# Early attention with a third score buffer, and the MLP's first norms and weights in space of their own

## The chip, the core and the metric

The kernel runs on one core of one Trainium2 chip. Five engines take their instructions in order, each from its own queue: PE (TensorE, matrix products and transposes), DVE (VectorE), ACT (ScalarE), POOL (GpSimd) and SP (SyncE, which issues nearly all DMAs). SBUF is the on-chip memory; PSUM, with eight banks, takes what PE produces. The metric is the device time of one execution in microseconds.

## The reference

Three layers follow each other, in float32, for 4 batches of 576 tokens:

```
scores = q k^T / 8                  # 4 batches x 8 heads, 576 x 576, head size 64
scores below (row maximum - tau) are masked; softmax; times v     -> x (4, 576, 512)
u  = x + real(fft over tokens and channels of x)
un = layer norm of u (no weights)
x  = u + relu(un @ w_ch1) @ w_ch2                                 # 512 -> 2048 -> 512
theta = x @ w_theta
u  = x + w_tok_r (x cos theta) + w_tok_i (x sin theta)            # mix over tokens
out = u + relu(u @ w_ch)
```

The MLP's and the last layer's weights come as float64.

## The kernel before

**Precision.** Most products use a float32 operand split in a high part (rounded to the matmul's format) and a low part (the rest), and add three products: high by high, high by low, low by high. So each operand costs an ACT copy (`hi`) and a DVE or POOL subtraction (`lo`).

**Attention.** The 32 heads are worked in 16 pairs. A pair's q and k are loaded (`raw`), split, and placed by 12 SBUF-to-SBUF DMAs in tiles L (q), H and X (high and low of k); each of `raw`, L, H, X has two buffers (`load_qk`, L293). A pair has 9 score tiles of 128 queries by 576 keys (`tile_ops`, L434). A tile goes: PE makes the scores in a PSUM buffer `ps` of two banks (L455, L456); DVE takes the negated maximum (L465); ACT the exponential (L470); DVE or POOL the bound, maximum less tau (L474, L476); DVE masks and sums (L481), after which `ps` is free; PE transposes the result (L488); ACT copies it from PSUM (L497). There are two `ps` buffers. All other PSUM results share four banks with the tag "O". When a pair's tiles are there, PE multiplies by v (L556) and DVE scales into `xT` (L561).

**Transform.** Each four pairs make one batch, whose two-dimensional transform (`fft`, L635) follows beside the next batch's pairs: POOL folds tokens and channels (L660 to L701; in the last batch the fold of the last pair may run on DVE), some extra rows go by DMA (L706), PE does two stages (L760 to L799), DVE joins them (L839, L843) and adds x (L817 to L821), and SP stores `u`. The last batch's transform has no later pairs beside it.

**MLP.** `channel_mlp` (L971) works 5 chunks of up to four 128-token tiles through 16 weight units. Chunk 0 is the tokens of batch 0, whose `u` is stored long before the pairs end. `norm` (L1068) loads a tile of `u`, DVE takes statistics (L1081, L1082), POOL the inverse root (L1086, L1087), DVE scales (L1091), PE transposes (L1096), ACT and DVE split (L1103, L1107). `widen` (L981) makes float32 of a unit of float64 weights by bit operations: ACT takes the magnitude of the high words (L999), DVE sets a floor (L1003), shifts and masks (L1007), sets the sign (L1011) and the low bits (L1015); ACT and POOL or DVE then split (L1034, L1037). A unit (`unit`, L1122) is 12 matmuls (L1134), relu and split (L1139, L1143) and a second product (L1154 to L1156) that adds into the two `ps` buffers.

**Space.** SBUF is handed over in three steps: when all pairs have their scores ("scores done"), the space of q and k becomes part "a" of the MLP's space; after the last pair ("attention done") part "b"; after the last transform ("fft done") part "c". The table `PART` (L1536) says which tile is in which part. The tiles of the norms (`un`, `bs`, `mv`), chunk 0's operands (`b16`, `b17`) and the buffers of the widening (`raw2`, `v0`, `v1`) are all in "a", so neither norms nor widening can begin before "scores done".

**Order.** The order on each engine is fixed when the program is built. `Plan` (L99) holds every operation with a cost, a priority and what it needs; `schedule` (L137) runs a model of the engines with these costs and picks, per engine, the lowest priority that can start. The engines then wait only on semaphores. `SHIFT` (L1552, L1671) is a long list of corrections that are added to priorities. Two operations that are listed in `PORT` for DVE and POOL are not put side by side.

Of the kernel before, what the change touches and what calls it, by code (L numbers as in the profile page):

```python
# [98 lines left out]
class Plan:  # L99
# [163 lines left out]

def attention_and_fft(pl, tc, ident, tb, pss, left, middle, right, qk, vv, cfk, cst, csr, u_d):
# [95 lines left out]
    def load_first():  # L360
# [7 lines left out]
        def dma(tag, h, o, n):  # L368
            def fn(e):
                for half, q in enumerate((e, nc.scalar)):  # L370
                    q.dma_start(loc[tag][64 * half:64 * half + 64, h * n:h * n + n], qk[0][64 * h:64 * h + 64, o:o + n])
            return fn
# [57 lines left out]
    def pair(p):  # L430
# [3 lines left out]
        def tile_ops(idx):  # L434
# [66 lines left out]
            ps, P, T = ("ps", k), ("P", (p, couple)), ("O", "T", k)  # L501
# [43 lines left out]
        def pv_ops(half, g):  # L545
# [3 lines left out]
            b, j = divmod(p, 4)  # L549
# [8 lines left out]
            def mul(e):  # L558
                if (j, half) == (0, 0):
# [9 lines left out]
            after = [("pv", k), ("Rc", p, half)] + ([("mu", p)] if half else []) + ([("mul", 4 * b)] if j else [])  # L569
            made = [xT] if (j, half) == (0, 0) else []  # L570
# [64 lines left out]
    def fft(b):  # L635
# [9 lines left out]
        def gtile(kind, j):  # L645
            return ("g1" if j else "g0", (b, kind, j))

        def mult(n, j):
            return (("POOL", pool(n)), ("DVE", dve(n))) if b == B - 1 and j == 3 else (("POOL", pool(n)),)

        def at(kind, j):
            return pr(9 * (4 * b + j) + FOLD_AT + "eo".index(kind), 10)
# [318 lines left out]
def channel_mlp(pl, tc, ident, tb, pss, P2, wf, u_d, x3_d, w3, w3_d):  # L971

    for t, n in dict(raw2=2, v0=1, v1=1, sh=1, un=2, hh=2, hl=2).items():
# [7 lines left out]
    def widen(key, src, n, prio):  # L981

        loc = {}
        vt = f"v{count[0] % 2}"
# [928 lines left out]
```

## Time and profile before

| what | us |
|---|---|
| median of 3 runs (lowest, highest) | 994.16 (993.51, 994.80) |
| the profiled execution, its own time | 994.31 |
| its span | 992.2 |
| PE busy | 957.0 (96%) |
| DVE busy | 643.3 (65%) |
| ACT busy | 445.4 (45%) |
| POOL busy | 219.2 (22%) |

The span runs from the first to the last instruction of the trace; busy time is the union of an engine's instructions, without its waits. The page cuts the span in 40 slices of 24.8 us; each digit is a busy share in tenths, 9 meaning 90% or more, and PEclk the granted TensorE clock in tenths of full speed. Score tiles run up to about slice 12, the end of the transforms and the start of the MLP lie in slices 13 and 14, the MLP reaches to about slice 31, and the last layer takes the rest.

### The profile page before, as it was taken

Reading aid. Unit: us, or ns where it says so; the run is one execution under the profiler, and the core shown is the slowest. Engines: PE = TensorE matmul, PEld = TensorE weight load, DVE = VectorE, ACT = ScalarE, POOL = GpSimd, SP = SyncE. Lnnn points to the kernel's source line nnn. Section 1 sums busy time; section 2 is a strip of 40 time slices with the busy share of each in tenths; the row PEclk is TensorE's granted clock in tenths of the full one; section 3 lists DMA queues with packets and bytes.
Section 4 is the critical chain, followed back from the end, with each engine's and each line's share of the span. In section 5 each row is a group of like instructions: output and inputs, shape, how many; then the busy total and the mean of one; then the engine's idle time right before and its main releaser. Section 6 shows DMA issues by size and latency. Waiting matters only on the chain.

```text
span 992.2 us, 16044 instructions
## 1 busy us (share of the span) xinstructions
PE 957.0 (96%) x5904; PEld 828.6 (84%) x5904; DVE 643.3 (65%) x1276; ACT 445.4 (45%) x845; POOL 219.2 (22%) x405
## 2 busy tenths in 40 slices
PE   6889999999999689999999999999999999999998
PEld 6667888887887578888888888898898999999998
DVE  6778888888888899985662442311255476776733
ACT  6678787787777344441331121111134333453410
POOL 3476565556454310021000000000000001100100
PEclk9999999999999899999999999999999999999999
DMA  7796656665652555555451461200316301111011
GB/s 191 199 229 163 184 147 167 181 161 147 151 134 83 168 178 172 180 188 183 172 191 38 156 209 54 75 1 1 127 55 245 106 23 52 40 35 57 23 37 48
DMA packets 49982, 122.86 MB, mean 124 GB/s; under 512 B 7089, under 2 KB 11761, under 8 KB 49521
## 3 DMA queue, kind: packets, MB, share of 16 engines
q1 hardware_dynamic: 48720, 117.84, 39.9%
q0 software_dynamic: 720, 2.76, 1.2%
q10 hardware_dynamic: 464, 1.25, 0.5%
q8 instruction: 47, 0.77, 0.3%
q14 instruction: 31, 0.25, 0.1%
HBM read 69.58 MB, written 23.66 MB: 94 GB/s over the span
## 4 chain that ended last, share of the span: by engine, by line
PE 86%; DVE 4%; DMA 4%; ACT 2%; issue 1%; SPq 1%; POOL 1%; DVEq 0%; POOLq 0%
PE h L1134 20%; PE y L1409 12%; PE acc L1155 7%; PE acc L1156 7%; PE acc L1154 7%; PE O L556 7%; PE f L1473 5%; PE th L1285 5%; PE T L488 4%; PE ps L455 4%; PE ps L456 3%; DMA raw<-in_qk 2%; ACT P L470 1%; DVE c L465 1%; DMA X<-raw 1%
## 5 line engine op out<-in xcount | busy, mean ns | idle before, releaser
L1134 PE MATMUL h<-uh,w 128*128 128x512 f32 (+1 forms) x640 | 198.5, 371 | 0.1
L1139 ACT ACTIVATE hh<-h 128x512 fp32r<-128x512 f32 (+1 forms) x80 | 44.4, 556 | 246.2 <-PE acc L1155 189.7
L1143 DVE SCALAR_TENSOR_TENSOR hl<-h,hh 128x512 fp32r<-128x512 f32 (+1 forms) x80 | 50.7, 636 | 146.0 <-ACT hh L1139 136.2
L1134 PEld LDWEIGHTS h<-uh,w 128*128 128x128 f32 x640 | 118.9, 188 | 17.4 <-issue 0.2
L470 ACT ACTIVATE P<-ps,c 128x576 f32<-128x576 f32 x144 | 106.6, 749 | 40.8 <-DVE c L465 37.9
L481 DVE SCALAR_TENSOR_TENSOR P<-ps,c,P 128x576 f32<-128x576 f32 x144 | 115.5, 814 | 13.4 <-ACT P L470 7.9
L465 DVE TENSOR_REDUCE c<-ps 128x1 f32<-128x576 f32 x144 | 106.8, 753 | 26.8 <-PE ps L456 25.0
L1134 PE MATMUL h<-ul,w 128*128 128x512 f32 (+1 forms) x320 | 118.4, 370 | 0.0
L1154 PE MATMUL acc<-w,hh 128*128 128x512 f32 x288 | 114.3, 397 | 0.0
L1156 PE MATMUL acc<-w,hl 128*128 128x512 f32 x288 | 113.2, 393 | 0.0
L1155 PE MATMUL acc<-w,hh 128*128 128x512 f32 x288 | 113.2, 393 | 0.0
L455 PE MATMUL ps<-H,L 128*128 128x288 f32 x320 | 99.3, 328 | 12.0 <-DVE P L481 10.9
L1409 PE MATMUL y<-w,z 128*128 128x288 f32 x768 | 110.6, 296 | 0.1
L1409 PEld LDWEIGHTS y<-w,z 128*128 128x128 f32 x768 | 104.6, 188 | 1.1 <-issue 0.3
L456 PE MATMUL ps<-X,L 128*128 128x288 f32 x320 | 89.4, 297 | 0.5 <-DVE X L403 0.5
L488 PE MATMUL T<-ident,P 128*128 128x128 f32 x576 | 82.2, 274 | 4.4 <-DVE P L481 1.9
L497 ACT COPY pt<-T 128x512 f32<-128x512 f32 (+1 forms) x160 | 82.3, 554 | 6.3 <-PE T L488 5.2
L556 PE MATMUL O<-pt,vr 128*64 128x320 f32 (+1 forms) x640 | 84.7, 411 | 0.0
L455 PEld LDWEIGHTS ps<-H,L 128*128 128x128 f32 x320 | 61.2, 191 | 24.4 <-issue 12.8
L488 PEld LDWEIGHTS T<-ident,P 128*128 128x128 f32 x576 | 67.4, 141 | 6.8 <-issue 1.9
L556 PEld LDWEIGHTS O<-pt,vr 128*64 128x64 f32 x640 | 43.1, 136 | 30.6 <-issue 3.7
L1134 PEld LDWEIGHTS h<-ul,w 128*128 128x128 f32 x320 | 60.1, 188 | 9.3 <-DVE ul L1107 0.3
(381 smaller groups left out, 1623.0 us busy)
## 6 DMA issues: line engine op xcount, KB each, us to landing
H<-hs SPq DMA_DIRECT2D x60, 160.0 KB
X<-raw SPq DMA_DIRECT2D x60, 160.0 KB
raw<-in_qk SPq DMA_DIRECT2D x14, 608.0 KB
vr<-in_vv SPq DMA_DIRECT2D x16, 384.0 KB
w<-w_d SPq DMA_DIRECT2D x6, 992.0 KB
mu<-u_d SPq DMA_DIRECT2D x18, 256.0 KB
ru<-u_d SPq DMA_DIRECT2D x18, 256.0 KB
x_d<-ru SPq DMA_DIRECT2D x18, 256.0 KB
```

The lines of the kernel that those rows point to most:

```text
L455: e.matmul(ps[:, half, :HS], L[:, qo:qo + 128], H[:, ko:ko + HS], start=(j == 0), stop=False)
L456: e.matmul(ps[:, half, :HS], L[:, qo:qo + 128], X[:, ko:ko + HS], start=False, stop=(j == n - 1))
L465: e.tensor_reduce(loc["c4"][:, 0:1], loc["ps"][:, :, :HS], axis=AXES.XY, op=ALU.max, negate=True)
L470: e.activation(halves(), loc["ps"][:, :, :HS], AF.Exp, bias=loc["c4"][:, 0:1], scale=1.0)
L481: e.scalar_tensor_tensor(halves(), loc["ps"][:, :, :HS], loc["c4"][:, 1:2], halves(), op0=ALU.is_ge, op1=ALU.mult, accum_out=st["sums"][:, ...
L488: e.transpose(T[:, kt * 128:(kt + 1) * 128], P[:, kt * 128:(kt + 1) * 128], ident[:])
L556: e.matmul(O[64 * h:64 * h + 64, :n], w, x, start=(kt == 0), stop=(kt == 4))
L1134: e.matmul(loc["ps"][:, :n], a, x[:, c, :n], start=(k == 0), stop=(k == 11))
L1154: e.matmul(a, hh[:, q], wh, start=(f == 0), stop=False)
L1155: e.matmul(a, hh[:, q], wl, start=False, stop=False)
L1156: e.matmul(a, hl[:, q], wh, start=False, stop=(f == NF - 1))
L1409: e.matmul(loc["ps"][:, half, :HS], z[:, cs], w, start=(n == 0 and m == 0), stop=(n == 8 and m == 2))
```

## The change

- Score tiles 0 to 35 (four pairs) have a third score buffer, `p2`: every third tile uses it. It is made of two of the four "O" banks, which are held until the mask of tile 35 and then given back (`two_more`).
- The pairs of each batch come in the order 3, 2, 1, 0 (`heads`), and with them the operations of the fold; the extra rows are taken from the pairs that now come first.
- A part "e" of SBUF is opened at the start. It holds the norms' tiles, chunk 0's operands and buffers `rawe`, `ve` for the first weight unit. The norms' loads no longer wait for "scores done"; the first unit's load waits for the first score tile of pair 12 in place of it. The descriptor space for POOL's DMAs is set to 1024.
- The widening has four steps for five: ACT scales the high words by 2^-112, POOL or DVE reduces the high word to its sign, DVE joins it with the low bits, DVE shifts and joins.
- The norm's scale may run on ACT, for which POOL makes one more value.
- The second block of `SHIFT` is replaced, so the planned order changes everywhere.

```diff
-        return self.banks[tag].tile(shape, F32, tag=f"{tag}{i}", name=name)
+        return (self.more if tag == "O" and i < 2 else self.banks[tag]).tile(shape, F32, tag=f"{tag}{i}", name=name)
...
+def heads(p):
+    return p + 3 - 2 * (p % 4)
...
-            e.dma_start(loc["raw"][:], qk[p])
...
+            third = 9 * p + idx < THREE and (9 * p + idx) % 3 == 2
...
-                ps = pss.tile([128, 2, 512], F32, tag="ps", name=f"ps{p}_{idx}")
+                ps = (pl.third if third else pss).tile([128, 2, 512], F32, tag="p2" if third else "ps", name=f"ps{p}_{idx}")
...
-            ps, P, T = ("ps", k), ("P", (p, couple)), ("O", "T", k)
+            ps, P, T = ("p2" if third else "ps", k), ("P", (p, couple)), ("O", "T", k)
...
-            b, j = divmod(p, 4)
+            b, j = divmod(heads(p), 4)
...
-            return ("g1" if j else "g0", (b, kind, j))
+            return ("g1" if j < 3 else "g0", (b, kind, j))
...
-            return (("POOL", pool(n)), ("DVE", dve(n))) if b == B - 1 and j == 3 else (("POOL", pool(n)),)
+            return (("POOL", pool(n)), ("DVE", dve(n))) if b == B - 1 and j == 0 else (("POOL", pool(n)),)
...
-            return pr(9 * (4 * b + j) + FOLD_AT + "eo".index(kind), 10)
+            return pr(9 * heads(4 * b + j) + FOLD_AT + "eo".index(kind), 10)
...
-            p0 = at(kind, j) + 0.02
-            pl.op(("ge", k), "SP", 1080, p0, extra, [("f2", (b, kind, j)), ("ez", b)], (),
+            p0 = at(kind, a) + 0.02
+            pl.op(("ge", k), "SP", 1080, at(kind, j) + 0.02, extra, [("f2", (b, kind, j)), ("ez", b)], (),
                   [g2, ex], delay=2500)
-            pl.op(("g", k), mult(ng, j), 0, p0 + 0.01, both, [("f2", (b, kind, j)), ("f2", (b, kind, a))], (), [g, g2])
+            pl.op(("g", k), mult(ng, a), 0, p0 + 0.01, both, [("f2", (b, kind, j)), ("f2", (b, kind, a))], (), [g, g2])
...
-            p0 = at("o", 3) + 0.02
-            pl.op(("ez", b), "POOL", 80, at("e", 2), extra_zero, (), [ex])
+            p0 = at("o", 2) + 0.02
+            pl.op(("ez", b), "POOL", 80, at("e", 3), extra_zero, (), [ex])
...
+THREE = 36
...
+        rt, vt = ("raw2", f"v{count[0] % 2}") if count[0] else ("rawe", "ve")
...
-            loc["raw"] = new("raw2", [128, 1024, 2], f"raw{key}", I32)
+            loc["raw"] = new(rt, [128, 1024, 2], f"raw{key}", I32)
...
-        def magnitude(e):
+        def rescale(e):
             loc["v"] = new(vt, [128, 1024], f"v{key}", I32)[:, :n]
-            e.activation(f32(loc["v"]), f32(loc["hw"]), AF.Abs)
-
-        def floor(e):
+            e.activation(f32(loc["v"]), f32(loc["hw"]), AF.Copy, scale=2.0 ** -112)
+
+        def sign(e):
+            h = f32(loc["hw"])
+            if e is nc.vector:
+                e.tensor_scalar(h, h, 0.0, None, op0=ALU.mult)
+            else:
+                e.tensor_mul(h, h, tb[:, 6:7].to_broadcast([128, n]))
+
+        def low(e):
+            e.scalar_tensor_tensor(loc["lw"], loc["lw"], 29, loc["hw"], op0=ALU.logical_shift_right, op1=ALU.bitwise_or)
+
+        def join(e):
             v = loc["v"]
-            e.tensor_scalar(f32(v), f32(v), 2.0 ** -15, None, op0=ALU.max)
-
-        def mantissa(e):
-            v = loc["v"]
-            e.tensor_scalar(v, v, 3, 0x3FFFFFF8, op0=ALU.logical_shift_left, op1=ALU.bitwise_and)
-
-        def sign(e):
-            v = loc["v"]
-            e.scalar_tensor_tensor(v, loc["hw"], -0x40000000, v, op0=ALU.bitwise_and, op1=ALU.bitwise_or)
-
-        def low(e):
-            v = loc["v"]
-            e.scalar_tensor_tensor(v, loc["lw"], 29, v, op0=ALU.logical_shift_right, op1=ALU.bitwise_or)
-
-        raw, v = ("raw2", key), (vt, key)
-        pl.op(("ca", key), None, 0, prio[0], begin, ["scores done"], [raw])
+            e.scalar_tensor_tensor(v, v, 3, loc["lw"], op0=ALU.logical_shift_left, op1=ALU.bitwise_or)
+
+        raw, v = (rt, key), (vt, key)
+        pl.op(("ca", key), None, 0, prio[0], begin, ["scores done"] if rt == "raw2" else [("S", (12, 0))], [raw])
         for i in range(2):
             pl.op(("cl", key, i), "SP", n * 1.55, prio[0], load(i), [("ca", key)], (), [raw], delay=2500)
-        pl.op(("c0", key), "ACT", act(n, False) + 80, prio[1], magnitude, [("cl", key, i) for i in range(2)], [v], [raw])
-        pl.op(("c1", key), "DVE", dve(n / 2), prio[2], floor, [("c0", key)], (), [v])
-        pl.op(("c2", key), "DVE", dve(n / 2), prio[2], mantissa, [("c1", key)], (), [v])
-        pl.op(("c3", key), "DVE", dve(n), prio[2], sign, [("c2", key)], (), [raw, v])
-        pl.op(("c4", key), "DVE", dve(n), prio[2], low, [("c3", key)], (), [raw, v])
+        pl.op(("c0", key), "ACT", act(n, False) + 80, prio[1], rescale, [("cl", key, i) for i in range(2)], [v], [raw])
+        pl.op(("c1", key), (("POOL", pool(n)), ("DVE", dve(n))), 0, prio[1], sign, [("c0", key)], (), [raw])
+        pl.op(("c2", key), "DVE", dve(n), prio[2], low, [("c1", key)], (), [raw])
+        pl.op(("c4", key), "DVE", dve(n), prio[2], join, [("c2", key)], (), [raw, v])
         return loc, v
...
-        pl.op(("wh", f), "ACT", act(1024, False), p0 - 1.5, hi, [("c4", ("w", f))] + (["fft done" if f >= NFA else "attention done"] if f else []), [slot],
+        pl.op(("wh", f), "ACT", act(1024, False), p0 - 1.5, hi, [("c4", ("w", f))] + (["fft done" if f >= NFA else "attention done"] if f else ["scores done"]), [slot],
...
+            e.tensor_scalar(mv[:, 1:2], mv[:, 0:1], -1.0, mv[:, 3:4], op0=ALU.mult, op1=ALU.mult)
...
+            if e is nc.scalar:
+                e.activation(u[:], u[:], AF.Identity, scale=mv[:, 3:4], bias=mv[:, 1:2])
+                return
             e.tensor_scalar(u[:], u[:], mv[:, 0:1], mv[:, 3:4], op0=ALU.subtract, op1=ALU.mult)
...
-        pl.op(("nl", k), "SP", 800, p0, load, ["scores done"] + stored(t), [u], delay=2500)
+        pl.op(("nl", k), "SP", 800, p0, load, stored(t), [u], delay=2500)
         pl.op(("n0", k), "DVE", 830, p0 + 1, stats, [("nl", k)], (), [u])
-        pl.op(("n1", k), "POOL", 820, p0 + 1, root, [("n0", k)])
-        pl.op(("n2", k), "DVE", 460, p0 + 2, scale, [("n1", k)], (), [u])
+        pl.op(("n1", k), "POOL", 985, p0 + 1, root, [("n0", k)])
...
-PART = {t: "a" for t in ("raw2", "v0", "v1", "un", "b16", "b17", "b0", "bs", "mv")}
+PART = {t: "a" for t in ("raw2", "v0", "v1", "b0")}
+PART.update({t: "e" for t in ("un", "b16", "b17", "bs", "mv", "rawe", "ve")})
...
 SHIFT += (
-    (('Rc', 13, 0), -94.12), (('Rc', 7, 1), -347.32), (('Rc', 8, 0), -290.69), (('Rc', None, 0), -37.05),
...
+    (('Rc',), -35.28), (('Rc', 14, 1), -54.55), (('Rc', 3, 0), -50.41), (('Rc', 7, 1), -115.81),
...
+    (('n0',), -20.29), (('n0', 0, 0), -904.08), (('n0', None, 0), -11.28), (('n3', 0, 2), -26.61),
+    (('n3', 2, 2), -15.94), (('n4',), -8.83), (('n4', 0, 0), -871.81), (('n5', 0, 1), -917.67),
...
             pl.tag("ps", 2)
+            pl.tag("p2", 1)
             pl.tag("O", 4, banks)
+            pl.third = top.enter_context(tc.tile_pool(name="third", bufs=1, space=PSUM, reuse_waits="tile"))
+
+            def two_more(e):
+                top.close()
+                pl.more = top.enter_context(tc.tile_pool(name="more", bufs=1, space=PSUM, reuse_waits="tile"))
+
+            held = [("O", "held", i) for i in range(2)]
+            pl.op("third", None, 0, -100, lambda e: None, (), held)
+            pl.op("two more", None, 0, -99, two_more,
+                  ["third"] + [("mask", divmod(n, 9)) for n in range(THREE) if n % 3 == 2], (), held)
             left, middle, right, late = Pools(tc, "left"), Pools(tc, "left"), Pools(tc, "right"), Late(tc, pl)
+            late.open("e")
             attention_and_fft(pl, tc, ident, tb, pss, left, middle, right, qk, vv, cfk, cst, csr, u_d)
...
             scores = [o["name"] for o in pl.ops if any(t[0] in RIGHT_TAGS for t in o["use"])]
...
-    nc = bacc.Bacc("TRN2", target_bir_lowering=False, num_devices=1)
+    nc = bacc.Bacc("TRN2", target_bir_lowering=False, num_devices=1, dynamic_dma_scratch_size=1024)
```

## Rows read from the trace of the kernel before

**Rows 1.** Stretches: us; busy us of PE, PEld, DVE, ACT, POOL; clock; DMA; GB/s.
```profile
0.00:25.00 25.00, 16.69 (x97) 15.74 (x98) 16.16 (x38) 15.85 (x28) 9.92 (x19) 0.93 0.73 192
25.00:75.00 50.00, 41.81 (x314) 32.63 (x313) 38.83 (x90) 35.52 (x70) 28.22 (x51) 1.00 0.88 214
75.00:125.00 50.00, 47.89 (x371) 38.57 (x369) 43.21 (x98) 39.69 (x86) 28.69 (x55) 1.00 0.69 174
125.00:325.00 200.00, 197.76 (x1554) 163.37 (x1554) 169.76 (x398) 152.00 (x321) 106.39 (x232) 1.00 0.57 148
325.00:375.00 50.00, 39.36 (x227) 34.12 (x226) 48.70 (x94) 20.52 (x33) 12.98 (x12) 0.90 0.52 167
375.00:975.00 600.00, 599.90 (x3252) 530.82 (x3251) 321.86 (x545) 180.84 (x307) 32.99 (x39) 1.00 0.30 100
975.00:992.20 17.20, 13.59 (x103) 13.36 (x102) 4.83 (x18) 0.95 (x4) 0.00 (x0) 1.00 0.16 52
```
**Rows 2.** Waits of PE, 0 to 100 us: us in total, times, longest.
```profile
PE ps L455 <- DVE P L481: 9.9, 8, 2.8
```
**Rows 3.** Waits of SP's queue, 0 to 110 us: total, times, longest.
```profile
SPq L332 <- PE ps L456: 10.7, 5, 7.8
```
**Rows 4.** The chain of waits, 0 to 110 us: start, length, what.
```profile
47.79 7.78 DMA L<-raw
55.58 7.94 DMA X<-raw
```
**Rows 5.** One line's instructions (L455), 25 to 75 us: PE, PEld, clock, DMA, GB/s.
```profile
25.00:75.00 50.00, 16.18 (x54) 9.93 (x53) 1.00 0.88 214
```
**Rows 6.** Waits of PE, 318 to 360 us, the longest.
```profile
PE xt L810 <- DVE dm L843: 4.7, 1, 4.7
```
**Rows 7.** Groups of DVE, 318 to 358 us: xcount | busy us, mean ns | idle before.
```profile
L1091 DVE TENSOR_SCALAR mu<-mu,mv 128x512 f32<-128x512 f32 x4 | 4.2, 1052 | 0.2 <-DMA raw('w', 0)_4626<-in_wf 0.2
L1081 DVE BATCH_NORM_STATS2 bs<-mu 128x6 f32<-128x512 f32 x6 | 4.1, 684 | 0.0
L1107 DVE TENSOR_TENSOR ul<-uT,uh 128x512 fp32r<-128x512 f32 x4 | 2.6, 679 | 0.0
...
L1011 DVE SCALAR_TENSOR_TENSOR v('w', 0)_4796<-raw('w', 0)_4626,v('w', 0)_4796 128x1024 int32<-128x1024 int32 x1 | 1.2, 1215 | 0.0
...
L1015 DVE SCALAR_TENSOR_TENSOR v('w', 0)_4796<-raw('w', 0)_4626,v('w', 0)_4796 128x1024 int32<-128x1024 int32 x1 | 1.2, 1192 | 0.0
...
L1007 DVE TENSOR_SCALAR v('w', 0)_4796<-v('w', 0)_4796 128x1024 int32<-128x1024 int32 x1 | 0.7, 686 | 0.0
```
**Rows 8.** The chain of waits, the first MLP matmul.
```profile
354.83 0.47 PE h L1134
```
**Rows 9.** Stretches of 2 us in the middle; columns as in rows 1.
```profile
332.00:334.00 2.00, 2.00 (x11) 1.92 (x10) 2.00 (x2) 0.12 (x1) 1.43 (x1) 0.50 0.29 66
...
342.00:344.00 2.00, 0.62 (x3) 0.62 (x4) 1.90 (x6) 1.98 (x2) 0.80 (x2) 0.50 0.44 129
344.00:346.00 2.00, 2.00 (x11) 2.00 (x10) 1.77 (x4) 0.00 (x0) 0.00 (x0) 0.50 0.97 340
346.00:348.00 2.00, 1.93 (x10) 1.53 (x9) 1.32 (x3) 0.38 (x1) 0.00 (x0) 0.50 0.52 195
```
**Rows 10.** DMA issues by POOL: count, KB each, median us to landing.
```profile
cfs<-in_cfk POOLq DMA_DIRECT2D x2, 516.0 KB, 7.2
...
ctr<-in_csr POOLq DMA_DIRECT2D x1, 640.0 KB, 9.5
```
**Rows 11.** Timeline, 337 to 341 us: start, length, instruction.
```profile
337.02 1.22 DVE L1011 SCALAR_TENSOR_TENSOR v('w', 1)_4816<-raw('w', 1)_4627,v('w', 1)_4816 128x1024 int32<-128x1024 int32 x1
337.54 2.91 POOL L1037 TENSOR_TENSOR w<-v('w', 0)_4796,w 128x1024 fp32r<-128x1024 f32 x1 [0.63 <-ACT w L1034]
338.15 2.58 DVE L1091 TENSOR_SCALAR mu<-mu,mv 128x512 f32<-128x512 f32 x1
```
**Rows 12.** Waits of DVE, 200 to 325 us.
```profile
DVE u L817 <- DMA u_d<-u: 2.5, 2, 2.0
```

More of the change, by code (lines that the diff above doesn't have):

```diff
@@ L370, in fn @@
                 for half, q in enumerate((e, nc.scalar)):
[L371 removed]
+                    q.dma_start(loc[tag][64 * half:64 * half + 64, h * n:h * n + n], qk[heads(0)][64 * h:64 * h + 64, o:o + n])
             return fn
@@ L558, in mul @@
             def mul(e):
-                if (j, half) == (0, 0):
+                if p % 4 == 0 and not half:
                     xTs[b] = new("xT", [128, 4, S], f"xT{b}")
@@ L568, in pv_ops @@
                   [("vr", p), ("pt5", p, 0), ("pt5", p, 1), (f"p0{half}", p), (f"p1{half}", p)])
-            after = [("pv", k), ("Rc", p, half)] + ([("mu", p)] if half else []) + ([("mul", 4 * b)] if j else [])
-            made = [xT] if (j, half) == (0, 0) else []
+            after = [("pv", k), ("Rc", p, half)] + ([("mu", p)] if half else []) + ([("mul", 4 * b)] if p % 4 else [])
+            made = [xT] if p % 4 == 0 and not half else []
             pl.op(("mul" if half else "mu", p), "DVE", dve(n), pr(g + 1, 7.5), mul, after, made,
@@ L669, in again @@
                 t = G["t", kind, j]
-                g = G[kind, j] = new("g1" if j else "g0", [128, 290], f"g{kind}{b}_{j}")
+                g = G[kind, j] = new("g1" if j < 3 else "g0", [128, 290], f"g{kind}{b}_{j}")
                 if kind == "e":
@@ L971, in channel_mlp @@
 def channel_mlp(pl, tc, ident, tb, pss, P2, wf, u_d, x3_d, w3, w3_d):
-    for t, n in dict(raw2=2, v0=1, v1=1, sh=1, un=2, hh=2, hl=2).items():
+    nc = tc.nc
+    for t, n in dict(raw2=2, rawe=1, ve=1, v0=1, v1=1, sh=1, un=2, hh=2, hl=2).items():
         pl.tag(t, n)
@@ L1111, in norm @@
         cs = [(a, ("c", ci)), (b, ("c", ci))]
-        pl.op(("nl", k), "SP", 800, p0, load, ["scores done"] + stored(t), [u], delay=2500)
+        pl.op(("nl", k), "SP", 800, p0, load, stored(t), [u], delay=2500)
         pl.op(("n0", k), "DVE", 830, p0 + 1, stats, [("nl", k)], (), [u])
-        pl.op(("n1", k), "POOL", 820, p0 + 1, root, [("n0", k)])
-        pl.op(("n2", k), "DVE", 460, p0 + 2, scale, [("n1", k)], (), [u])
+        pl.op(("n1", k), "POOL", 985, p0 + 1, root, [("n0", k)])
+        pl.op(("n2", k), (("ACT", act(512, False)), ("DVE", 460)), 0, p0 + 2, scale, [("n1", k)], (), [u])
         pl.op(("n3", k), "PE", 428, p0 + 3, turn, [("n2", k)] + ([("first", (ci - 2, NF - 1))] if ci > 1 else []) +
@@ L1750 @@
-    (('turn', None, None, 1), -6.3), (('turn', None, 'r'), -1.34), (('uh',), 84.74), (('us',), -104.35),
-    (('us', 1), 67.22), (('wl', 0), 54.14), (('x3',), 13.27), (('x3', 6), 43.93), (('x3s', 17), -9.75),
-    (('z',), 27.65),
[14 rows of a table added]
+    (('bound', 15, 7), -65.59), (('bound', 2), 38.66), (('bound', 5, 3), -52.26), (('bound', 6), -14.44),
+    (('bound', 6, 7), -53.12), (('bound', None, 1), 34.41), (('bound', None, 3), 15.7), (('bound', None, 4), -89.68),
[3 rows of a table added]
+    (('evac', None, 1), 83.37), (('exp',), -42.45), (('exp', 0, 5), -2.05), (('exp', 0, 6), 165.12),
@@ new lines @@
+    (('exp', 0, 7), 0.56), (('exp', 1, 8), 146.16), (('exp', 12, 3), 75.58), (('exp', 15, 1), 82.64),
+    (('exp', 2, 6), 44.13), (('exp', 3, 3), 39.1), (('exp', 3, 5), 0.9), (('exp', None, 3), 43.29),
[10 rows of a table added]
+    (('first',), 3.69), (('first', 0, 10), -28.82), (('first', 2), -23.47), (('fl',), 48.42),
[11 rows of a table added]
+    (('mask', 13, 2), 890.74), (('mask', 9, 5), 29.16), (('mask', None, 3), -27.12), (('mask', None, 5), -39.66),
+    (('mask', None, 6), 16.99), (('mask', None, 8), -11.78), (('mix',), 10.46), (('mix', 0, 0, (0, 1), 0), -29.7),
@@ new lines @@
+    (('mix', None, 1, (0, 1), 0), -8.66), (('mix', None, None, (0, 1), 3), 50.43),
+    (('mix', None, None, None, 1), -17.31), (('mix', None, None, None, 6), -20.32), (('mul', 12), -37.16),
[5 rows of a table added]
+    (('second', 2, 9), 33.13), (('second', 4, 4), 20.1), (('table',), 28.65), (('tk',), 31.54), (('tl', 0), -1.51),
+    (('tt',), 14.86), (('tt', 3), -32.21), (('turn', 0, 0), -33.48), (('turn', 1), 40.49), (('turn', 10, 6), 76.2),
+    (('turn', 10, 'r', 1), 25.85), (('turn', 10, 'r', 2), -16.69), (('turn', 11, 1), -3.58), (('turn', 11, 7), 77.35),
@@ new lines @@
+    (('turn', 11, 'r', 0), 16.46), (('turn', 12), -1.66), (('turn', 12, 3), -11.83), (('turn', 12, 4), 12.06),
+    (('turn', 13, 3), 1.06), (('turn', 13, 4), 886.61), (('turn', 14, 1), -1.71), (('turn', 14, 3), 27.2),
+    (('turn', 14, 4), 24.84), (('turn', 14, 8), 59.49), (('turn', 15, 4), 31.82), (('turn', 15, 'r'), 4.5),
+    (('turn', 2, 1), -0.71), (('turn', 2, 4), 22.73), (('turn', 3, 1), -16.45), (('turn', 3, 2), -9.96),
+    (('turn', 3, 5), 3.37), (('turn', 3, 6), 12.46), (('turn', 3, 8), 18.97), (('turn', 3, 'r', 1), 16.73),
@@ new lines @@
+    (('turn', 4, 4), 21.15), (('turn', 5), -0.64), (('turn', 5, 4), 20.36), (('turn', 5, 7), -18.52),
+    (('turn', 6, 6), 25.17), (('turn', 7, 'r', 2), -26.24), (('turn', 8, 2), -6.02), (('turn', 8, 3), -0.96),
+    (('turn', 8, 4), 16.16), (('turn', 8, 5), 38.27), (('turn', 9, 7), -28.1), (('turn', None, 0), 7.2),
+    (('turn', None, 1), -4.93), (('turn', None, 2), 0.49), (('turn', None, 4), 2.54), (('turn', None, 6), -1.59),
+    (('turn', None, 7), -2.48), (('turn', None, None, 2), -1.46), (('turn', None, 'r', 0), 30.44), (('uh',), 73.54),
@@ L1791, in body @@
             scores = [o["name"] for o in pl.ops if any(t[0] in RIGHT_TAGS for t in o["use"])]
-            attention = [o["name"] for o in pl.ops if any(t[0] not in LEFT_TAGS and t[0] not in ("ps", "O")
+            attention = [o["name"] for o in pl.ops if any(t[0] not in LEFT_TAGS and t[0] not in ("ps", "p2", "O")
                                                           for t in o["use"]) or o["name"][0] in ("guard", "inv", "Rt", "bound")]
```

44 lines of the change are left out of this document (13 added, 31 removed), and 92 rows, old and new, of the table SHIFT.

## The prediction

> **What bounds the kernel now.** I read the page, then its busy time in stretches, then the waits of PE, the chain of waits and the timeline of the two places where PE is not full. The stretches [rows 1] show a kernel that is bound by PE nearly everywhere: from 375 to 975 us PE is busy 599.90 of 600, from 125 to 325 it is busy 197.76 of 200. Nothing the change does in those stretches can gain much there; it can only lose. PE is idle for 8.31 us in the first 25, 8.19 from 25 to 75, 2.11 from 75 to 125, 2.24 from 125 to 325, 10.64 from 325 to 375, and 3.61 in the tail. That is 35.2 us in all and the whole prize, with what the clock takes beside it.
>
> At the start PE waits for a score buffer. In the first 100 us it stands 9.9 us, in eight waits, at the first score matmul of a tile until the mask of an earlier tile (DVE, L481) gives its PSUM buffer back [rows 2]. Two buffers serve a chain score, maximum, exponential, mask, and PE runs dry behind them. But the loads are near too: SP stood 10.7 us before the placing of a pair until the scores of an earlier pair let go of its tile L [rows 3], and the chain of waits holds 7.78 us for L and 7.94 us for X back to back [rows 4]. So one pair's placing takes at least 15.7 us (47.79 to 63.52), while in 25 to 75 PE did 54 of these matmuls, 20 a pair, so a pair took 18.5 us [rows 5].
>
> In the middle, 325 to 375, the last pairs are over, the last batch's transform is a chain across PE, ACT and DVE, and the MLP can't start. PE's longest wait is 4.7 us for a transform step on DVE (L843) [rows 6]. DVE is busy 48.70 of these 50 us [rows 1]: it also does chunk 0's layer norms and the widening of the first weight unit, which had to wait for the space of the scores [rows 7]. The first MLP matmul starts at 354.83 [rows 8]. Having run thin, PE was also slowed: the granted clock is 0.50 (1.2 of 2.4 GHz) in 332 to 334 and in 342 to 348 [rows 9].
>
> **The change part by part.** The sum is made against the profiled execution: 994.3 us, a span of 992.2 and 2.1 around it. The median of the runs shown, 994.16, lies 0.15 below, so both give the same forecast.
>
> (a) Third score buffer in the first 36 tiles, with two fewer banks for everything else. It can remove at most the 9.9 us of [rows 2]. It can't bring the next pair sooner than its placing: 18.5 less 15.7 is 2.8 us a pair, over the 2.5 to 3 pairs of that stretch 7 to 8 us. What is late next is that placing, and it itself starts when an earlier pair ends, so part comes back. Against it stand the two remaining banks: a transpose must wait until the copy before last has left, and a value product holds its bank until its multiply. No row shows two banks at work. I bound the part by 9.9 gained and, by the same eight waits moving from score buffers to these banks in all four pairs, 8 lost. I take a gain of 5, half of the waits, nearest to [rows 2].
>
> (b) Layer norms of chunk 0 and weight unit 0 leave the middle. The groups of DVE price them [rows 7]: statistics 0.68 each, so with the scale (4.2 for four) and the low part (2.6 for four) about 4 x 0.68 + 4.2 + 2.6 = 9.5, and the unit's four steps 0.7 + 0.7 + 1.2 + 1.2 = 3.8 (L1003 is as long as the L1007 shown). Some of the statistics were already done before 325, so about 11 us of DVE leave a stretch in which DVE is full. The last batch's steps then run when their inputs are there, and PE has unit 0 (twelve matmuls and a second half with as many columns) as filler in the gaps that remain. What can come back is the idle 10.64 and the clock: PE's busy time at 0.50 in [rows 9] is 2.00, 0.62, 2.00 and 1.93, half of which is 3.3. Together 13.9. The transform's chain itself stays and unit 1 still waits for the scores to end before it loads, so I leave 3.5 of it: a gain of 10.4. Bounds: 0, if these operations run no earlier, and 13.9.
>
> (c) The same work now lies in 125 to 325. There DVE has 200 - 169.76 = 30 us free and ACT 48 [rows 1], so 11 us fit by their sum, and the four groups of transposes only change place on a PE that is full in either. But each operation put ahead of a maximum or mask can hold PE for its own length, and PE has only 2.24 us of idle to swallow that. Between 0 and 11, I take 2, nearest to the large slack.
>
> (d) Widening in four steps instead of five. DVE loses two steps of 0.7 and keeps two of 1.2; the new sign step runs on POOL or, at about 1.2, on DVE. From 375 on PE is full, so there it is worth nothing; in 325 to 375 it is inside (b).
>
> (e) Pairs in the order 3, 2, 1, 0 of each batch. The extra rows of the transform are ready before the last pair. PE's longest wait in the middle is on DVE [rows 6], not on those rows, so 0; its most would be that 4.7, which (b) holds already. The smaller descriptor space: each table load takes 7.2 to 9.5 us from POOL's issue to landing [rows 10]. If POOL issues on as before it costs 0, which I take; if POOL were held until each landing, five loads hold it 4 x 7.2 + 9.5 = 38 us, 22 of them in POOL's idle time of 25 to 75 [rows 1], 16 beyond.
>
> Sum: 994.3 - 5 - 10.4 + 2 = 980.9, forecast 981.
>
> **A rule against it.** While POOL made the low part of unit 0 (2.91 us from 337.54, begun during a DVE step with two SBUF inputs), the DVE scale that began at 338.15 lasted 2.58 us, where the other three average (4.2 - 2.58) / 3 = 0.54 [rows 7, 11]. A POOL pass over 1024 columns thus can hold DVE for over 2 us. The Trainium skill, "SBUF — State Buffer", section "Who interferes with whom", says that a VectorE operation with two SBUF inputs and a GpSimd operation that reads SBUF exclude each other, whichever began second waiting; by that the sign step on POOL blocks the two remaining DVE steps, which both have two such inputs. The trace agrees for the scale; no row shows such a two-input step begun during a POOL read.
>
> **The rivals.**
> - POOL holds DVE in the middle. Of the units widened in 325 to 375 about five have a sign step on POOL, over 1024 columns as the 2.91 us row; if DVE waits for most of each, 11 us of DVE return, as much as (b) takes out, and of (b) about a third is left, the filler of unit 0: 994.3 - 5 + 2 - 3.4 = 988. For it: [rows 11]. Against it: what waits most in the hole reads PSUM.
> - The start gives nothing or a little less, because two banks or the placing take over: 986, up to 994 at the bound of (a). For it: [rows 3 to 5].
> - All comes back: 994.3 - 9.9 - 13.9 = 970.5. For it: the slack in [rows 1]; against it, the chain of the last batch.
> - Slower: the static order is held by loads that land late. In 125 to 325 DVE reads the four norm tiles and ACT two halves of weight unit 0 straight from new loads, and behind each in the queue stand the maxima, exponentials and masks on which PE waits. DVE already stood 2.5 us there, in two waits, for a store [rows 12]. A transfer among the pair loads took 7.78 or 7.94 us [rows 4]; a load that lands 3.5 us after its reader's turn costs that much of PE, and six cost 21: 994.3 - 15.4 + 21 = 1000. It decides from 15.4 / 6 = 2.6 us a load on.
> - Slower by (e): POOL held by the table loads, 981 + 16 = 997. No row shows the smaller space at work.
>
> **How the numbers follow.** Forecast 0.56; POOL holds DVE 0.14; nothing at the start 0.10; all 0.06; late loads 0.10; table loads 0.04. The predicted time is 981. The range 969 to 994 takes in the forecast's own terms, the first two rivals and part of the third, and leaves the slower cases out. A run can tell 0.2%, 2 us, from no change. Faster: the first four without the end of the second, 0.82; same 0.04; slower 0.14.
>
> **What would show it.** (a): the waits of score matmuls on masks in 0 to 100 at about half or less, PE idle in 0 to 125 near 13.5 instead of 18.6. (b): the first MLP matmul well before 340, PE busy in the 50 us after the last pair near 46, no granted clock of 0.50 there. (c): PE idle between 125 and the last pair under 5. (d): DVE steps of the widening no longer than 1.3. Wrong would be: DVE waiting for loads amid the pairs, waits of transposes on copies in the first four pairs, or a hole that only moved.

## The result, and the profile after

The changed kernel takes 984.38 us (median of 4 runs, 983.68 to 985.88), the kernel before beside it 994.3. The ratio is 0.9905, with a 95% interval of 0.9892 to 0.9917. The profiled execution took 984.21 us with a span of 982.1, 10.1 less than before. A second profile of the same kernel, in another comparison, has a span of 982.6 and a ratio of 0.9904 [0.9880, 0.9927].

The same stretches as in [rows 1], of the changed kernel (us; busy us of PE, PEld, DVE, ACT, POOL; granted clock; DMA; GB/s):
```profile
0.00:25.00 25.00, 17.08 (x95) 15.62 (x95) 16.62 (x39) 16.00 (x28) 9.17 (x20) 0.93 0.74 200
25.00:75.00 50.00, 46.06 (x341) 35.72 (x341) 41.84 (x101) 39.11 (x78) 28.49 (x48) 1.00 0.90 214
75.00:125.00 50.00, 48.97 (x377) 38.61 (x379) 41.23 (x95) 40.31 (x87) 34.70 (x62) 1.00 0.74 188
125.00:325.00 200.00, 193.61 (x1514) 161.41 (x1512) 174.23 (x413) 152.81 (x318) 114.41 (x236) 1.00 0.57 150
325.00:375.00 50.00, 48.10 (x281) 39.41 (x278) 42.59 (x66) 21.20 (x33) 16.36 (x13) 1.00 0.54 179
375.00:975.00 600.00, 599.33 (x3280) 531.15 (x3279) 298.73 (x510) 182.72 (x315) 58.73 (x59) 1.00 0.29 97
975.00:982.10 7.10, 3.50 (x27) 3.27 (x25) 1.57 (x6) 0.00 (x0) 0.00 (x0) 1.00 0.26 83
```
PE's idle time is each stretch less PE's busy time. Against [rows 1] it went from 18.61 to 12.89 us in the first 125, from 2.24 up to 6.39 in 125 to 325, from 10.64 to 1.90 in 325 to 375, and from 0.10 to 0.67 in 375 to 975. Together that is 9.75 less; PE's busy time is 0.35 less. These make the 10.1. The clock of 0.50 in the middle [rows 9] is gone (325 to 375 has 1.00).

The waits of PE in the first 100 us (total, times, longest) answer [rows 2]:
```profile
PE ps L460 <- DVE P L486: 4.6, 4, 3.5
PE T L493 <- ACT pt L502: 2.3, 6, 0.6
...
PE ps L460 <- DVE c L479: 1.2, 1, 1.2
PE R L601 <- ACT pt L502: 1.2, 2, 1.0
PE T L531 <- ACT pt L502: 0.9, 1, 0.9
```
The wait for a score buffer fell from 9.9 to 4.6 us, or to 5.8 with the 1.2 that the view puts down to the bound (L479), at the same matmul. In its place stand waits of a transpose for a bank that ACT has yet to copy out: 2.3, 1.2 and 0.9, where the kernel before had 0.8 and 0.7 of that kind in the same stretch. I put them down to the two banks that were given away; t27 below, which takes these back after three pairs, has no such wait in 62.5 to 125, where the changed kernel has 1.2. SP's wait to place a pair until the scores let go of L [rows 3] is now short:
```profile
SPq L336 <- PE ps L461: 3.3, 2, 2.9
```
The first MLP matmul, in the timeline (start, length), against 354.83 in [rows 8]:
```profile
329.98 0.48 PE L1142 MATMUL h<-uh,w 128*128 128x512 f32 x1
```

### The profile page after: what moved, and what is told of

It is laid out like the page before. It is cut to its first block, busy times and chain, and to the rows that moved or that the text cites. A ratio compares the mean times of both kernels' runs of the same rounds, so it can differ in the third digit from the quotient of the medians.

```text
span 982.1 us, 15994 instructions
## 1 busy us (share of the span) xinstructions
PE 956.6 (97%) x5904; PEld 825.2 (84%) x5904; DVE 616.8 (63%) x1226; ACT 452.1 (46%) x856; POOL 261.9 (27%) x436
## 4 chain that ended last, share of the span: by engine, by line
PE 83%; DVE 6%; ACT 5%; issue 2%; DMA 2%; POOL 1%; SPq 0%; DVEq 0%; ACTq 0%
PE h L1142 18%; PE y L1417 12%; PE O L561 7%; PE acc L1163 6%; PE acc L1162 6%; PE acc L1164 6%; PE f L1481 5%; PE th L1293 5%; PE T L493 4%; PE ps L460 4%; PE ps L461 3%; ACT P L475 2%; DVE c L470 2%; ACT pt L502 1%; DMA mu<-u_d 1%
## 5 line engine op out<-in xcount | busy, mean ns | idle before, releaser
L486 DVE SCALAR_TENSOR_TENSOR P<-ps,c,P 128x576 f32<-128x576 f32 x144 | 114.9, 813 | 10.7 <-ACT P L475 8.3
L1417 PE MATMUL y<-w,z 128*128 128x288 f32 x768 | 108.1, 295 | 0.0
L561 PE MATMUL O<-pt,vr 128*64 128x256 f32 (+1 forms) x640 | 84.7, 411 | 0.0
```

The costliest lines, as they stand in the source:

```text
L486: e.scalar_tensor_tensor(halves(), loc["ps"][:, :, :HS], loc["c4"][:, 1:2], halves(), op0=ALU.is_ge, op1=ALU.mult, accum_out=st["sums"][:, ...
L561: e.matmul(O[64 * h:64 * h + 64, :n], w, x, start=(kt == 0), stop=(kt == 4))
L1417: e.matmul(loc["ps"][:, half, :HS], z[:, cs], w, start=(n == 0 and m == 0), stop=(n == 8 and m == 2))
```

## The experiments

Each kernel starts from the changed one. "Planned anew" means that the program orders the operations afresh, with the corrections that were made for the changed kernel; "same order" keeps every engine's order.

**e2: the early start undone** (planned anew).
```diff
-load, stored(t), [u], delay=2500)
+load, ["scores done"] + stored(t), [u], delay=2500)
-["scores done"] if rt == "raw2" else [("S", (12, 0))]
+["scores done"]
```


> The loads of the norms and of weight unit 0 wait for the last score tile again, as in the kernel before; all else is the changed kernel, planned anew. If the early start is what filled the middle, PE's idle time in 325 to 375 goes from 1.90 back to 9 to 12 us, the first MLP matmul from 330 back to about 350, and the time to 992 to 996 (984.4 + 10, less the 2 to 4 that 125 to 325 gets back). If the hole closed for another reason (fewer widening steps, the order of the pairs), the first MLP matmul stays before 340 and the time within 2 us of 984. Either way 0 to 125 keeps its idle 12.9.

Measured: 999.93 us, ratio 1.0058 [1.0038, 1.0078], slower than the kernel before. The first MLP matmul starts at 364.96. The middle of e2, and the stretch before it:
```profile
325.00:375.00 50.00, 37.76 (x196) 31.80 (x193) 39.93 (x72) 22.50 (x34) 25.23 (x30) 0.80 0.50 169
125.00:325.00 200.00, 195.12 (x1522) 161.24 (x1519) 166.50 (x398) 147.09 (x310) 106.27 (x221) 1.00 0.54 142
```
The hole is back: 12.24 us idle for 1.90, and a granted clock of 0.80 on the mean. The clock costs nearly as much as the idle: PE's busy time over the whole run is 965.42 for 956.65, 8.8 more. So, under these corrections, the early start is a condition of the gain. My number was too small, since I had priced the idle and left out the time that PE then runs at the lower clock. Nor did 125 to 325 get back the 2 to 4 us that I had expected: it still idles 4.88 us, though the first of the moved statistics runs at 319.4.

**t9 and t27: the third buffer for one pair, and for three** (planned anew).
```diff
-THREE = 36
+THREE = 9        # t27: 27
```


> The third score buffer serves only the first 9 tiles (the first pair) instead of 36; planned anew. Theory: the buffer gains where pairs 1 and 2 run, so PE's idle time in 25 to 75 goes from 3.94 back to 7 to 9 and the time to 987 to 990. Rival: the gain of the start is made in the first pair, or by something else than the buffer (the order of pairs, later work pulled forward): idle in 25 to 75 stays under 5 and the time within 2 us of 984.4.

> The third score buffer serves the first 27 tiles (three pairs) in place of 36; planned anew. Theory: the buffer pays in the pairs in which it stands, so PE's idle in 25 to 62.5 is as in the changed kernel (2.8) and that of 62.5 to 100 grows from 2.1 by 2 to 4 (it was 4.2 in the kernel before); time 986 to 989. Rival: t9 lost its 13 us by a plan whose corrections fit another kernel; then the start here is either as in the changed kernel (0 to 125 idle near 12.9) or as poor as in t9 (27.0), whichever pairs have the buffer.

Measured: t9 999.45 us, ratio 1.0049 [1.0034, 1.0063]; t27 992.21, 0.9979 [0.9963, 0.9996]. Stretches of the kernel before, of the changed kernel, of t27 and of t9, in this order:
```profile
25.00:62.50 37.50, 32.17 (x242) 24.73 (x241) 29.20 (x69) 25.45 (x51) 19.61 (x34) 1.00 0.86 209
```
```profile
25.00:62.50 37.50, 34.66 (x252) 26.15 (x253) 29.95 (x72) 27.21 (x56) 19.57 (x33) 1.00 0.92 213
62.50:100.00 37.50, 35.37 (x268) 27.89 (x267) 32.99 (x80) 30.78 (x66) 25.46 (x45) 1.00 0.77 204
```
```profile
25.00:62.50 37.50, 35.23 (x256) 26.73 (x257) 30.05 (x71) 27.18 (x57) 19.88 (x35) 1.00 0.93 223
62.50:100.00 37.50, 32.12 (x240) 25.26 (x239) 27.74 (x68) 27.60 (x57) 23.43 (x46) 0.95 0.73 189
```
```profile
25.00:62.50 37.50, 29.57 (x219) 22.20 (x219) 27.68 (x65) 24.38 (x48) 13.63 (x19) 1.00 0.82 209
```
With the buffer in pairs one to three, t27 idles 2.27 us in 25 to 62.5, as the changed kernel does (2.84); t9, without it, idles 7.93. From 62.5 on, where t27 lacks it too, it idles 5.38 for 2.13. So the buffer pays in the pairs in which it stands. But its price can't be read off: t9 with two buffers is worse than the kernel before with two (5.33 in 25 to 62.5), so part of t9's loss, and I take it of t27's, is a plan whose corrections were made for three. That would explain why both expected times were too low; no run separates it.

**e5: every sign step on DVE** (same order).
```diff
-            if e is nc.vector:
-                e.tensor_scalar(h, h, 0.0, None, op0=ALU.mult)
-            else:
-                e.tensor_mul(h, h, tb[:, 6:7].to_broadcast([128, n]))
+            nc.vector.tensor_scalar(h, h, 0.0, None, op0=ALU.mult)
```


> Same order on every engine but for one thing: the sign step of all weight units is emitted on DVE, the ones that POOL had too. If POOL's sign step holds DVE's two widening steps, the shift-and-join steps of 2.83 and 2.10 us near 350 fall to about 1.2. Theory: those lie off PE's path in the middle and where PE is full, so the time stays within 1.5 us of 984.4. Rival (POOL holds DVE on PE's path): PE's idle 1.90 in 325 to 375 falls and the time drops by 2 us or more.

Measured: 982.63 us, 0.9878 [0.9861, 0.9895]; the profiled span is 982.1, that of the changed kernel. The timeline of the changed kernel at the sign step on POOL (L1013), then the same steps of e5:
```profile
347.13 3.00 POOL L1013 TENSOR_TENSOR raw('w', 4)_5006<-raw('w', 4)_5006,tb 128x1024 f32<-128x1024 f32 x1 [8.50 <-ACT v('w', 4)_5083 L1006]
347.15 1.20 DVE L1016 SCALAR_TENSOR_TENSOR raw('w', 3)_4910<-raw('w', 3)_4910 128x1024 int32<-128x1024 int32 x1
348.39 2.83 DVE L1020 SCALAR_TENSOR_TENSOR v('w', 3)_5050<-v('w', 3)_5050,raw('w', 3)_4910 128x1024 int32<-128x1024 int32 x1
```
```profile
350.34 0.68 DVE L1010 TENSOR_SCALAR raw('w', 4)_5006<-raw('w', 4)_5006 128x1024 f32<-128x1024 f32 x1
350.94 1.21 DVE L1017 SCALAR_TENSOR_TENSOR v('w', 3)_5050<-v('w', 3)_5050,raw('w', 3)_4910 128x1024 int32<-128x1024 int32 x1
```
DVE's join of unit 3 took 2.83 us beside POOL's step and takes 1.21 without it; POOL's own step took 3.00, where the shortest of this size took 1.92. The Trainium skill, "SBUF — State Buffer", section "Who interferes with whom", has the two exclude each other, and the trace agrees. Unit 4's join stayed at 2.10, beside POOL's low part of unit 3. PE doesn't feel it in the middle: its idle in 325 to 375 is 2.23, so the rival is out there. The time fell by 1.75 us, a little more than the 1.5 that my theory allowed; from 375 to 975 PE idles 0.09 for 0.67, and the profile, whose span is that of the changed kernel, explains no more. The intervals of the two ratios overlap, so that e5 is faster is not shown.

**e11 and e16: the old five steps, for all units, and for those after unit 7** (same order; the sign step's slot stays empty).
```diff
-e.scalar_tensor_tensor(loc["lw"], loc["lw"], 29, loc["hw"], op0=ALU.logical_shift_right, op1=ALU.bitwise_or)
+e.tensor_scalar(f32(v), f32(v), 2.0 ** -15, None, op0=ALU.max)
+e.tensor_scalar(v, v, 3, 0x3FFFFFF8, op0=ALU.logical_shift_left, op1=ALU.bitwise_and)
...
-e.scalar_tensor_tensor(v, v, 3, loc["lw"], op0=ALU.logical_shift_left, op1=ALU.bitwise_or)
+e.scalar_tensor_tensor(v, loc["hw"], -0x40000000, v, op0=ALU.bitwise_and, op1=ALU.bitwise_or)
+e.scalar_tensor_tensor(v, loc["lw"], 29, v, op0=ALU.logical_shift_right, op1=ALU.bitwise_or)
```


> Same order, but every weight unit is widened by the old steps: ACT takes the magnitude, POOL's or DVE's sign step is empty, and DVE does floor, mantissa (0.7 each), sign and low (1.2 each). Theory: four steps for five are worth nothing, since PE is full behind them: the time within 1 us of 984.4, PE's idle in 325 to 375 under 3 (1.90 with four). Rival: DVE is near its limit in the middle (42.6 of 50 us busy), and 0.7 to 1.4 us more for each of the seven units widened there brings back 3 us or more of idle and a time of 987 or more.

> Same order; units 0 to 7 of the weights are widened by the new four steps, all later units and the last layer's weights by the old five, with the sign step's slot empty. If the 10 us that e11 cost come from the middle, where DVE is full and the units 1 to 7 are made, this stays within 1.5 us of the changed kernel (0.990 of before). Rival: DVE supplies weights just in time up to 450 us, and the later units cost as well: 987 or more, with idle of PE between 385 and 450.

Measured: e11 994.25 us, 0.9992 [0.9976, 1.0007]; e16 984.66, 0.9902 [0.9879, 0.9925]. Stretches of e11:
```profile
325.00:375.00 50.00, 45.62 (x264) 37.24 (x264) 40.97 (x66) 19.59 (x31) 10.36 (x12) 0.97 0.47 157
375.00:385.00 10.00, 8.03 (x39) 6.78 (x40) 9.31 (x13) 4.13 (x5) 2.40 (x1) 1.00 0.46 155
342.00:344.00 2.00, 0.72 (x6) 0.39 (x4) 1.97 (x3) 0.13 (x1) 0.00 (x0) 1.00 0.37 131
344.00:346.00 2.00, 0.64 (x3) 0.64 (x4) 1.94 (x4) 0.91 (x1) 0.00 (x0) 0.73 0.58 117
346.00:348.00 2.00, 2.00 (x11) 2.00 (x11) 1.75 (x4) 0.95 (x1) 0.00 (x0) 0.50 0.93 352
```
and its longest waits of PE in 325 to 390:
```profile
PE Xo L765 <- DVE xle L784: 2.6, 1, 2.6
PE xt L815 <- DVE hl L1150: 2.1, 1, 2.1
```
The whole gain of the change is gone, and e16 shows where: the later units cost nothing, so it is units 0 to 7. The unit's DVE steps are 0.7 + 0.7 + 1.2 + 1.2 in e11, and 0.7 + 1.2 + 1.2 in e5: one step of 0.7 us more a unit. Their places differ as well. The sign step's slot is empty, floor and shift stand where e5 has one later step, and sign and low bits where it has the last one. DVE's last steps of unit 1 and the transform step behind them, in e5 and then in e11 (other rows left out):
```profile
340.18 1.21 DVE L1017 SCALAR_TENSOR_TENSOR v('w', 1)_4906<-v('w', 1)_4906,raw('w', 1)_4764 128x1024 int32<-128x1024 int32 x1
...
342.45 0.42 DVE L784 TENSOR_TENSOR xle<-Xe,xhe 128x258 fp32r<-128x258 f32 x1
```
```profile
341.37 1.21 DVE L1018 SCALAR_TENSOR_TENSOR v('w', 1)_4908<-raw('w', 1)_4765,v('w', 1)_4908 128x1024 int32<-128x1024 int32 x1
342.61 1.23 DVE L1019 SCALAR_TENSOR_TENSOR v('w', 1)_4908<-raw('w', 1)_4765,v('w', 1)_4908 128x1024 int32<-128x1024 int32 x1
...
344.89 0.42 DVE L784 TENSOR_TENSOR xle<-Xe,xhe 128x258 fp32r<-128x258 f32 x1
```
Only units 2 and 1 are widened ahead of this hole. The transform's step comes 2.4 us later and PE waits 2.6 us for it; DVE is full from 342 to 346, and the clock falls to 0.50 behind the hole. The wait of 2.1 us is of the same kind, behind the last two steps of unit 6 (373.83 to 376.32). So it is the DVE steps of these units, ahead of work that PE needs, that bring most of the loss. Whether five steps would cost as much in an order made for five, no run tells. The profiled execution took 991.93, 2.3 less than the median: of its 8.1 us over the changed kernel's span, 4.5 are PE's idle time from 325 to 385 and 2.1 more busy time. My theory (worth nothing) was wrong, my rival right, with 10 us for its 3.

**e6, e14, e13: the moved work made nearly empty, one part of it, and one wait of it** (same order). e6 lets chunk 0's statistics and ACT scale and unit 0's sign, low and join steps work on 64 columns; e14 does so for unit 0's steps alone; e13 keeps all work and lets the scale of chunks 0 and 1 take constants.
```diff
+            lw, hw = (loc[i][:, :64] if rt == "rawe" else loc[i] for i in ("lw", "hw"))    # e6, e14
...
-                e.bn_stats(bs[:], loc["u"][:])
+                e.bn_stats(bs[:], loc["u"][:, :64] if ci == 0 else loc["u"][:])            # e6
...
-            u, mv = loc["u"], loc["mv"]
+            u, mv = loc["u"], loc["mv"] if ci > 1 else tb[:, 1:5]                          # e13
```


> Same order on every engine, but the work that was moved amid the pairs is made nearly empty: chunk 0's statistics and its scale on ACT, and unit 0's sign, low and join steps, work on 64 columns only (so chunk 0 and unit 0 give other values). Theory: these steps, standing ahead of exponentials and masks in in-order queues, cost PE about 4 us between 125 and 325; its idle time there then falls from 6.39 to 2.5 to 4 and the time to 980 to 982.5. Rival: the idle time comes from the new order itself (what waits for what), not from the length of the moved steps: idle stays at 5.5 to 6.5 and the time within 1 us of 984.4.

> Same order, but only weight unit 0's sign, low and join steps work on 64 of 1024 columns (unit 0 gives other values); the norms stay whole. In e6, where the norms were cut too, the idle of 125 to 325 fell by 2.2. If the length of the widening steps on DVE (0.7 + 1.2 + 1.2) was its cause, by holding a mask or POOL's inverse root, the idle falls by 1.5 or more here as well, in 250 to 290. If the norms on ACT were, it falls by under 0.7.

> Same order on every engine, all steps as long as before, but the scale of chunks 0 and 1 takes constants in place of the inverse root that POOL makes (so these two chunks are normalised wrongly): ACT no longer stands behind POOL. ACT stood 2.9 us there in three waits between 125 and 325. Theory: these waits, with exponentials behind them, are a good part of what 125 to 325 lost, so PE's idle time there falls from 6.39 by 1.5 to 2.5 and the time by 1.5 to 2.5. Rival: the length of the moved steps or the order alone makes the idle; then it falls by less than 0.7 and the time stays within 1 us of 984.4.

Measured, time and ratio, and idle of PE in 125 to 325 (6.39 in the changed kernel): e6 981.97, 0.9881 [0.9862, 0.9900], 4.21; e14 982.49, 0.9874 [0.9859, 0.9889], 4.83; e13 981.84, 0.9865 [0.9849, 0.9881], 5.08. The timeline of the changed kernel shows what all three cut (rows of other instructions left out):
```profile
265.90 1.22 DVE L1016 SCALAR_TENSOR_TENSOR raw('w', 0)_3539<-raw('w', 0)_3539 128x1024 int32<-128x1024 int32 x1
...
265.96 1.23 POOL L1090 TENSOR_SCALAR mv<-mv 128x1 f32<-128x1 f32 x1
267.27 0.55 POOL L1091 TENSOR_TENSOR mv<-mv,tb 128x1 f32<-128x1 f32 x1
267.95 0.27 POOL L1092 TENSOR_SCALAR mv<-mv 128x1 f32<-128x1 f32 x1
268.25 0.81 ACT L1097 ACTIVATE mu<-mu,mv 128x512 f32<-128x512 f32 x1 [1.20 <-POOL mv L1092]
269.08 1.37 ACT L475 ACTIVATE P<-ps,c 128x576 f32<-128x576 f32 x2
269.93 0.82 DVE L486 SCALAR_TENSOR_TENSOR P<-ps,c,P 128x576 f32<-128x576 f32 x1 [2.14 <-ACT P L475]
...
270.90 0.41 PE L531 MATMUL T<-ident,P 128*128 128x128 f32 x2 [1.69 <-DVE P L486]
```
Unit 0's low step on DVE (1.22) holds a POOL instruction of one element a partition for 1.23 us; ACT's scale waits 1.20 for POOL, the exponential stands behind it, DVE's mask waits 2.14, PE 1.69. The waits of PE in 250 to 290, of the changed kernel, of e14 and of e13:
```profile
PE T L531 <- DVE P L486: 1.7, 1, 1.7
PE ps L460 <- DVE P L486: 0.5, 2, 0.3
```
```profile
PE ps L460 <- DVE P L486: 0.6, 2, 0.3
PE T L531 <- DVE P L486: 0.6, 2, 0.4
```
```profile
PE ps L460 <- DVE P L486: 0.9, 3, 0.4
PE T L531 <- DVE P L486: 0.2, 1, 0.2
```
Shortening DVE's step (e14, where POOL's instruction takes 0.22) or freeing ACT from POOL (e13) takes away the same wait, so it is one chain and not two costs. It is worth 1.0 to 1.1 us of idle in 250 to 290 (2.20 in the changed kernel, 1.19 and 1.10 in e14 and e13), the two edits 1.3 to 1.6 in the whole stretch, and all that e6 made empty 2.2. About 2 of the 4.15 that this stretch lost remain in e6. The new order explains them better than what e6 left whole (transposes, splits, unit 0's first step on ACT): e2 has none of the moved work before 319.4 and idles 2.64 more than the kernel before. By the numbers that I had set, e14 met its 1.5, while e13's 1.31 and e6's 4.21 fall a little short of their theories. (e13 gained besides in its first 25 us, below.)

**e7, e15: POOL's root taken as later, without and with e5's edit** (planned anew), beside **the changed kernel once more**.
```diff
-pl.op(("n1", k), "POOL", 985, p0 + 1, root, [("n0", k)])
+pl.op(("n1", k), "POOL", 985, p0 + 1, root, [("n0", k)], delay=1500)
```


> The planner is told that POOL's inverse root is ready 1.5 us later than its own cost says, and plans anew; nothing else. If ACT's waits for the root are what the amid-pairs work costs, the plan puts ACT's scale later and the idle of 125 to 325 falls by 1.5 to 3, the time to 981 to 983. Rival: any new plan under corrections that were made for another one loses as much as in e2 and t9, whose stretch 375 on was full but whose middle or start opened: 986 or more.

> The changed kernel itself, once more, so that e15 is compared with it in the same call. Every theory expects 984 to 985, a ratio of 0.990 to before.

> e5 and e7 together: the plan that takes POOL's inverse root as ready 1.5 us later, and every sign step emitted on DVE. If the two gains are separate (e5 frees DVE of the 2.83 us step in the middle, e7 took 1.6 us of idle out of 125 to 325 but lost 1.1 from 375 on), the time is 981 to 983, 2 us or so under the changed kernel of this call, and PE's idle from 375 to 975 is under 1.7. Rival: what e7 lost from 375 on has nothing to do with the sign step, and the time is that of the changed kernel within 1 us.

Measured: e7 984.49 us, 0.9895 [0.9879, 0.9910]; the changed kernel 984.75, 0.9904 [0.9880, 0.9927]; e15 982.96, 0.9880 [0.9854, 0.9905]. In e7 the idle of 125 to 325 fell to 4.76 as expected, and 375 to 975 gave back 1.06 (1.73 idle), so its time stayed. e15 has both stretches at 5.01 and 0.75. With e5 it has the lowest ratio of the versions that keep all the work, but its interval overlaps that of the changed kernel: that it beats it is not shown. e7 also shows that not every new plan loses.

## Why the prediction was right, and where not

The sum came out 3.3 us too low (980.9 for 984.21). The sign held, and so did the range, which at 25 us is two and a half times as wide as the change is large.
- **(a) third buffer, -5:** PE's idle in 0 to 125 fell by 5.7. The score-buffer waits about halved (9.9 to 4.6, or 5.8) and the two banks took some 2.9 (4.4 for 1.5), both as the step had it: the sign that I had named for being wrong came, at a price that the gain carries. That placing is late next isn't seen: SP's wait for it fell from 10.7 to 3.3, I take it since the buffers turn faster.
- **(b) norms and unit 0 out of the middle, -10.4:** idle fell by 8.74, and the clock stayed at 1.00. But the 3.3 us that the sum's 13.9 put to the clock don't show: PE's busy time over the run fell by 0.35 only (by 1.5 in the second profile, 955.5), and where the rest went stays open. The part was costed too simply as work that leaves DVE: e2 shows that the early start is needed, e11 that it isn't enough.
- **(c) the same work amid the pairs, +2:** it was 4.15, the largest miss of the sum, and the idle of 6.39 is over the 5 that I had set as its sign. The mechanism (an operation ahead of an exponential or a mask holds PE) is the one shown in 261 to 271, but the wait runs through four engines, which slack by engine doesn't show. And I had taken the new order as free: about 2 us of it remain with most of the work made empty, and e2 idles 2.64 more than the kernel before without it.
- **(d) four steps, 0:** the step that failed. What the steps are worth in the middle was left to (b), whose sum holds unit 0's steps alone; those of units 1 to 7 were priced nowhere. There they decide: with the five put in the places of the four, the ratio goes from 0.9905 to 0.9992. From unit 8 on they are worth nothing, as said. That no step would exceed 1.3 us was wrong too (2.83, 2.10).
- **(e) order of the pairs, descriptor space, 0:** not tried alone. POOL issues each table load in 0.58 to 0.80 us, and isn't held.
- **Rivals:** POOL does hold DVE, off PE's path (e5), and in 325 to 375 it has one sign step (unit 4) for the five that were priced. The DVE scale of [rows 11] reads one tile of SBUF and isn't the two-input case; the join in e5 is. Nothing at the start is out by (a). The late loads exist (DVE waited 1.6 us for norm tiles in 125 to 325) but are far from their price of 21. All coming back failed on each of (a), (b) and (c).

Undoing (a), (b) or (d) costs 0.0144, 0.0153 and 0.0087 of the ratio, together four times the gain of 0.0095. The parts are not terms of a sum: each undo reopens a hole, I take it partly because the order was made for the whole, and in e2 and e11 the clock charges the hole once more.

## What to carry to other kernels

Where one in-order engine is nearly full across a gap of PE, price each of its steps there by the work of PE that stands behind it in the queue, up to the whole hole: one step of 0.7 us more a unit, with 1.2 us more just ahead of what PE waited for, cost 8 to 10 us, clock included, while the same steps were free from the ninth unit on, where PE had other work. Work moved into slack is charged by the longest chain of in-order queues that it joins, not by each engine's slack. And an undo under an order made for the whole says that a part is needed, not what it is worth.

## What the runs showed of the hardware that I had not expected

- A POOL instruction on one element a partition (L1090) took 1.23 us beside a DVE step with two SBUF inputs, and 0.22 at the median of its 18 times.
- DVE's sign step with one input was held as well: 1.97 us for 0.70, beside a POOL step that began 1 us earlier:
```profile
357.03 2.40 POOL L1041 TENSOR_TENSOR w<-v('w', 4)_5083,w 128x1024 fp32r<-128x1024 f32 x1 [2.25 <-ACT w L1038]
358.01 1.97 DVE L1011 TENSOR_SCALAR raw('w', 5)_5106<-raw('w', 5)_5106 128x1024 f32<-128x1024 f32 x1 [0.81 <-ACT v('w', 5)_5184 L1006]
```
- The granted clock of the first 25 us varied between runs that begin alike: 0.93 in both profiles of the changed kernel, 0.86 in e16 and 1.00 in e13, where PE was busy 15.52 us for 99 matmuls instead of 17.08 for 95 (16.10 for 95 in the second profile of the changed kernel). Four more matmuls in the same 25 us are by my estimate about 1 us (4 x 25 / 95; 0.7 by busy time alone), so that much of e13's time is not its edit, and single profiles are told apart here by stretches, not by spans.
